# Holding the weight loads of an attention + MLP kernel behind the third pair's k, with a re-measured schedule model

## The chip, the cores and the metric

The kernel runs on one core of a Trainium2 chip. The metric is device time in microseconds (us) of that core; lower is better. "Span" is the length of the one execution that was profiled; a run's time is about 1.7 us longer than its span. A run is called slow when it is more than 1.5% above the fastest run of the same kernel, otherwise fast.

In the profile lines PE is TensorE's matmuls, PEld its weight loads, DVE VectorE, ACT ScalarE, POOL GpSimd and SP the Sync engine. PEclk is the granted clock: the share of TensorE's full clock that the records show. The DMA share is the mean busy share of the core's 16 DMA engines as the profile counts it; it passes 1 here (1.24 from 11 to 12 us of the kernel before).

## The reference

Block-sparse attention (4 batches, 8 heads, 768 tokens, head size 64) is followed by a two-layer MLP with a gated activation. Inputs and outputs are fp32.

```python
def _attn_ref(q, k, v, sampled_blocks):        # q, k, v: (4, 8, 768, 64)
    scores = scale * np.matmul(q, k.transpose(0, 1, 3, 2))
    mask = ...                                  # neighbours, first and last blocks, 3 sampled blocks of 32
    scores = np.where(mask, scores, -1e9)
    ...                                         # softmax over keys
    return np.matmul(attn, v)

def _moe_ref(x, w_in, w_out, beta):             # x: (3072, 512), w_in: (512, 2048), w_out: (2048, 512)
    h = x @ w_in
    g = h * (1.0 / (1.0 + np.exp(-beta * h)))
    return g @ w_out
```

## The kernel before

The kernel works on pairs of heads. There are 16 pairs: four per batch. Per pair, k, q and v are loaded as fp32 by the Sync engine's hardware DMA queue, cast to fp16 by VectorE or GpSimd, and k and q are transposed ("turned"): for pairs 0 to 3 on TensorE, later by DMA. TensorE makes scores, ScalarE takes exponentials, VectorE applies the mask, TensorE multiplies by v. When a stretch of tokens is complete for all four pairs, the MLP follows: `w_in` matmuls (up-projection), tanh, product, `w_out` matmuls (down-projection).

The weights are 8.4 MB of fp32. GpSimd issues four loads of 2.1 MB each that also cast to fp16 (4.2 MB written). They go through the software DMA queue.

The emitted order is not written by hand. A list scheduler in Python (`order_of`) simulates engines, buffers and two DMA "wires" with constants of its own, and emits each engine's instructions in the order in which its model starts them. A constant of the model has an effect only by moving instructions.

```python
BIAS = {"mask": -29, ..., "load": 168, "cast": 123, "dma": -234, ...}   # (cut) priority offsets, ns
RATE = {"SP": 356.0, "POOL": 410.0}              # bytes per ns of the two wires
DMA_FIRST = {"SP": 1260.0, "POOL": 2000.0}       # ns from issue to first byte
SHARED = 60.0                                    # what SP gets while both run

    def add_weights(after):                      # after: a load of the second pair
        for i in range(2):
            def wi(i=i):
                nc.gpsimd.dma_start(out=w_in_sb[:, :, i * 1024:(i + 1) * 1024],
                                    in_=w_in_r[:, :, i * 1024:(i + 1) * 1024])
            w_in_of[i] = add("weights", "POOL", 1000, 0, wi,
                            deps=[after, (mask_of[1], -1e9)], moved=2097152, port=True)
        ...                                      # two more for w_out
    # later loads: k of pair 4 waits for w_out's first half, its q and v for the second half
    for x in range(NPAIR, len(pairs)):
        add_prep(x, (0, 1, 1) if x == NPAIR else (None, None, None))
```

The `after` dependency exists only in the model. Nothing in the emitted program makes GpSimd wait for that load, so the weight loads go out as soon as GpSimd gets to them: from 8.36 us in the trace before, right behind its three mask copies (7.01 to 8.42 us). Pairs 0 to 3 load k, the first 256 columns of q, then v; the rest of q for these four pairs is loaded after all of that.

The softmax here doesn't subtract the row's maximum and nothing guards it: scores larger than these inputs give would overflow.

Of the kernel before, what the change touches and what calls it, by code (L numbers as in the profile page):

```python
# [23 lines left out]
class Node:  # L24


    def __init__(self, kind, eng, dur, lat, emit, deps=(), take=(), use=(), moved=0,
# [10 lines left out]
        self.start = self.done = self.on = None  # L38


BIAS = {"mask": -29, "spread": 107, "beta": 401, "weights": 209, "load": 168, "cast": 123,
        "dma": -234, "turn": 72, "turn cp": 164, "sc": -30, "next sc": -209, "lone sc": 110,
        "ex": 138, "mk": 62, "av": 35, "norm": 5, "x turn": 26, "x cp": 78, "hp": 33, "op": 68,
        "op on": 83, "th": 123, "gm": -192, "osb": 149}

HOP = 60.0
SWITCH = 100.0
RATE = {"SP": 356.0, "POOL": 410.0}
DMA_FIRST = {"SP": 1260.0, "POOL": 2000.0}
DMA_LAST = 900.0  # L50
SHARED = 60.0

# [1 line left out]
def order_of(nodes, free, slots):  # L54

    free = dict(free)
    give = {p: [(0.0, s) for s in range(n)] for p, n in slots.items()}
    rows = 128
    wire = {"SP": 0.0, "POOL": 0.0}
    port = {"DVE": 0.0, "POOL": 0.0}  # L60
    left, after, at_dep = {}, {}, {}
    todo = []
    for n in nodes:
        left[n] = len(n.deps)
        at_dep[n] = n.at
        for d, x in n.deps:
            after.setdefault(d, []).append((n, x))
        if not n.deps:
            todo.append(n)
    out = []  # L70
    while todo:
        best = None
        for n in todo:
            ready = at_dep[n]
            want = {}
            for b in n.take:
                want[b.pool] = want.get(b.pool, 0) + 1
            ok = True
            for p, c in want.items():
                if len(give[p]) < c:  # L80
                    ok = False
                    break
                ready = max(ready, sorted(give[p])[c - 1][0])
            if not ok:
                continue
            for e in n.eng:
                n_start = max(ready, free[e])
                if n.port and e in port:
                    n_start = max(n_start, port["POOL" if e == "DVE" else "DVE"])
                bias = BIAS[n.kind]  # L90
                if n.rows == 64:
                    if rows == 64:
                        bias += BIAS["next sc"]
                    elif sum(t <= n_start for t, _ in give["sc"]) < 2:
                        bias += BIAS["lone sc"]
                key = (n_start + n.dur[e] - min(n.dur.values()) + bias, n.place)
                if best is None or key < best[0]:
                    best = (key, n, e, n_start)
        if best is None:
            raise RuntimeError("no node can start")  # L100
        _, n, e, start = best
        if e == "PE" and n.rows != rows:
            start, rows = start + SWITCH, n.rows
        n.on, n.start = e, start
        free[e] = start + n.dur[e]
        if n.port and e in port:
            port[e] = free[e]
        if n.moved:
            other = "POOL" if e == "SP" else "SP"
            t, rest, rate = max(wire[e], start + DMA_FIRST[e]), n.moved, RATE[e]  # L110
            if wire[other] > t:
                if e == "POOL":
                    t = wire[other]
                else:
                    both = min(rest, (wire[other] - t) * SHARED)
                    wire[other] += both / RATE[other]
                    t, rest = t + both / SHARED, rest - both
            wire[e] = t + rest / rate
            n.done = wire[e] + DMA_LAST
        else:  # L120
            n.done = free[e] + n.tail
        for b in n.take:
            t, b.slot = min(give[b.pool])
            give[b.pool].remove((t, b.slot))
        for b in n.use:
            b.users -= 1
            b.end = max(b.end, n.done)
            if b.users == 0:
                give[b.pool].append((b.end + HOP, b.slot))
        todo.remove(n)  # L130
        out.append(n)
        for m, x in after.get(n, ()):
            at_dep[m] = max(at_dep[m], n.done + HOP + x)
            left[m] -= 1
            if left[m] == 0:
                todo.append(m)
    if len(out) < len(nodes):
        raise RuntimeError("some nodes never become ready")
    return out
# [3 lines left out]
def kernel(  # L143
# [192 lines left out]
    N_PE_TURN = 4  # L336
    prep = {}

    w_in_of, w_out_of = {}, {}
    last_load = []  # L340

    def add_weights(after):
        for i in range(2):
            def wi(i=i):
                nc.gpsimd.dma_start(out=w_in_sb[:, :, i * 1024:(i + 1) * 1024],
                                    in_=w_in_r[:, :, i * 1024:(i + 1) * 1024])
            w_in_of[i] = add("weights", "POOL", 1000, 0, wi,
                            deps=[after, (mask_of[1], -1e9)], moved=2097152, port=True)
        for i in range(2):
            def wo(i=i):  # L350
                nc.gpsimd.dma_start(out=w_out_sb[:, i * 8:(i + 1) * 8, :],
                                    in_=w_out_r[:, i * 8:(i + 1) * 8, :])
            w_out_of[i] = add("weights", "POOL", 1200, 0, wo, deps=[(w_in_of[1], -1e9)],
                              moved=2097152, port=True)
# [4 lines left out]
    def add_load(nm, x, st, lo, hi, gate):  # L359
        b, j = pairs[x]  # L360
        src = {"k": k, "q": q, "v": v}[nm]

        def load():
            hg = src[b, 2 * j:2 * j + 2].rearrange("h (g p c) d -> p (h g) (c d)", g=NG, p=P)
            o = at(st).rearrange("p h (g c) -> p (h g) c", g=NG)
            if hi - lo == NC:
                nc.sync.dma_start(out=o, in_=hg)  # L367
            else:
                for g in range(lo // CG, hi // CG):
                    nc.sync.dma_start(out=o[:, g::NG], in_=hg[:, g::NG])  # L370
        deps = [(last_load[0], -1e9)] if last_load else []
        kw = {"take": [st]}
        if gate is not None:
            def shut():
                nc.gpsimd.tensor_copy(out=at(st)[0:1, 0, lo * D:lo * D + 1],
                                      in_=w_out_sb[0:1, gate * 8, 0:1])
            deps.append(add("weights", "POOL", 150, 50, shut, deps=[w_out_of[gate]], take=[st]))
            kw = {"use": [st]}
        last_load[:] = [add("load", "SP", 500 if hi - lo in (NC, CG) else 1000, 0, load, deps=deps,
                             moved=65536 * (hi - lo) + (500000 if x == 0 and nm == "v" else 0),  # L380
                             **kw)]
        return last_load[0]

    def add_cast(x, nm, st, dst, lo, hi, load):
        w = (hi - lo) * P

        def cast(eng):
            e = nc.vector.tensor_copy if eng == "DVE" else nc.gpsimd.tensor_copy
            src = at(st)[:, :, lo * D:hi * D].rearrange("p h (c d) -> p h c d", d=D)
            e(out=at(dst)[:, :, :, 0:D] if nm == "v" else by_chunk(dst, lo, hi),  # L390
              in_=src)
        return add("cast", ("DVE", "POOL"), {"DVE": 60 + 0.53 * w, "POOL": 50 + 0.94 * w}, 90, cast,
                   deps=[load], take=[dst], use=[st], port=True)

    def add_half(x, nm, kq, lo, hi, first, gate):

# [1 line left out]
        w = (hi - lo) * P  # L398
        st, s16 = Buf(f"st_{nm}"), Buf(f"s16_{nm}")
        load = add_load(nm, x, st, lo, hi, gate)  # L400
        c = add_cast(x, nm, st, s16, lo, hi, load)
        if x >= N_PE_TURN:
            def turn():
# [19 lines left out]
    def add_prep(x, gates=(None, None, None)):  # L423
        kq, va, st = Buf("set"), Buf("va"), Buf("st_v")
        hi = Q1 // P if x < NPAIR else NC
        tk = add_half(x, "k", kq, 0, NC, None, gates[0])
        tq = add_half(x, "q", kq, 0, hi, tk, gates[1])
        lv = add_load("v", x, st, 0, NC, gates[2])
        cv = add_cast(x, "v", st, va, 0, NC, lv)
        prep[x] = {"kq": kq, "va": va, "k": tk, "q": tq, "q on": tq, "v": cv}  # L430
        return lv

    def add_rest(x):
        r = prep[x]
# [41 lines left out]
    def add_step(step):  # L476
        x, q0, sc, et, mm, ex, mk, masks = step
        r = prep[x]
        g = add("sc", "PE", 218, 180, mm, deps=[r["k"], r["q"] if q0 == 0 else r["q on"]],
                take=[sc], use=[r["kq"]], rows=64)  # L480
        e = add("ex", "ACT", 927, 100, ex, deps=[g], take=[et], use=[sc])
        return add("mk", "DVE", 612, 80, mk, deps=[e] + masks, use=[et], port=True)
# [118 lines left out]

    n_bh = add_mask()

    at_load = [add_prep(x) for x in range(NPAIR)]
    add_weights(at_load[1])
    for x in range(NPAIR):
        add_rest(x)
    for x in range(NPAIR, len(pairs)):
# [63 lines left out]
```

## Time and profile before

| | before |
|---|---|
| time, median of the runs first given | 307.5 us (305.45 to 307.69) |
| span of the profiled run | 303.9 us |
| TensorE busy | 269.2 us, so 34.7 us idle |
| TensorE busy in the first 40 us | 15.5 us |
| first `w_in` matmul | 51.5 us |

First the page of the kernel before: its span, the busy times, and two rows in 40 slices of 7.6 us (TensorE's busy tenths; the DMA share in tenths).

```profile
span 303.9 us, 6163 instructions
...
PE 269.2 (89%) x2455; PEld 140.8 (46%) x2455; DVE 211.2 (69%) x427; ACT 212.4 (70%) x276; POOL 31.8 (10%) x48
...
PE   5714079999987999998999999999999999999995
...
DMA  7999958519999996677212620112101111002002
...
```

TensorE is at 7 to 9 from the sixth slice on, and at 9 almost everywhere after the thirteenth. The holes are in slices 1 to 5, and there the DMA row is at 7 to 9. So the start waits for DMA and the rest is bound by TensorE.

The waits before 60 us (engine and its line, what released it, total us, times, longest):

```profile
...
engine line waited for: us in total, times, longest us
POOL s_q L390 <- DMA st_q<-in_q_dram: 28.4, 1, 28.4
ACT et L461 <- PE sc L453: 16.4, 5, 13.6
...
PE mm L412 <- DVE s_q L390: 11.9, 3, 8.2
...
```

Stretches of the kernel before: start and end in us, length, busy us of each engine with its number of instructions, granted clock, DMA share, GB/s.

```profile
...
core 0: us, PE busy (x) PEld busy (x) DVE busy (x) ACT busy (x) POOL busy (x), PEclk, DMA share, GB/s
10.00:11.00 1.00, 0.31 (x4) 0.21 (x3) 1.00 (x3) 0.36 (x1) 1.00 (x2) 1.00 1.22 291
11.00:12.00 1.00, 0.77 (x16) 0.71 (x14) 1.00 (x3) 0.00 (x0) 1.00 (x2) 1.00 1.24 266
12.00:13.00 1.00, 1.00 (x17) 1.00 (x15) 1.00 (x3) 0.00 (x0) 0.18 (x1) 1.00 1.12 218
...
30.00:35.00 5.00, 0.00 (x0) 0.00 (x0) 0.56 (x1) 0.00 (x0) 0.00 (x0) 1.00 1.20 215
0.00:40.00 40.00, 15.49 (x133) 9.52 (x135) 15.86 (x46) 12.13 (x15) 8.88 (x22) 1.00 1.08 223
...
```

The DMA moves about 290 GB/s until 11 us and 215 to 218 GB/s after 12 us. The change of level marks the moment at which weight traffic joins (these GB/s count written bytes; the page's software queue has 4.19 MB for the 8.4 MB of fp32 weights). Between 30 and 35 us TensorE does nothing.

Next, one v load, pair 3's (the tile view, limited to what is issued from 10.3 to 11.2 us), and the weights (the tile view of `w_in_sb` up to 75 us; each line gives count, durations, first and last start):

```profile
...
L367 SPq DMA_DIRECT2D st_v<-in_v_dram x1: 415/415/415, 10.8 to 10.8; - x1
...
DMA to landing us min/median/max: 20.4/20.4/20.4
```

```profile
...
L554 PE MATMUL mm<-xT_sb,w_in_sb x64: 269/273/283, 51.5 to 60.9; 128*128 128x256 f16 x64
L345 POOL DMA_DIRECT2D w_in_sb<-in_moe_w_in_dram x2: 748/833/918, 8.4 to 9.3; - x2
...
DMA to landing us min/median/max: 10.3/12.9/15.4
```

Pair 3's v needed 20.4 us from issue at 10.8 us to landing at 31.2 us, because it shares the DMA with the weights, which were issued from 8.4 us on. The `w_in` halves landed at 18.7 and 24.7 us, but the first `w_in` matmul comes at 51.5 us. The weights came early, and the data that the attention needs first came late.

### The profile page before, as it was taken

To read this page: it belongs to the slowest core of one execution; us is meant where nothing else is said; L and a number is where in the kernel's file an instruction comes from. 1 tells how busy PE (TensorE), PEld (TensorE's weight loads), DVE (VectorE), ACT (ScalarE), POOL (GpSimd) and SP (SyncE) were. 2 spreads that over 40 slices of the span, in tenths; PEclk is the share of its full clock that TensorE was granted. 3 is DMA by queue.
4 is the path that set the end of the run, shared out by engine and by line. 5 is a ranking of instruction groups with operands and counts; after the bars stand their busy time and mean duration, and the time that the engine had idled before them with its cause. 6 is when DMAs were issued, how large, how long until landed. Compare 5 with 4: busy or idle time off the path is not lost.

```text
span 303.9 us, 6163 instructions
## 1 busy us (share of the span) xinstructions
PE 269.2 (89%) x2455; PEld 140.8 (46%) x2455; DVE 211.2 (69%) x427; ACT 212.4 (70%) x276; POOL 31.8 (10%) x48
## 2 busy tenths in 40 slices
PE   5714079999987999998999999999999999999995
PEld 2503035665532536543645446455336364465742
DVE  5812169889985958897967778678887588762510
ACT  2533058999886668699788877787997689734621
POOL 5600032101133110123300001000000000000000
PEclk9999999999999999999999999999999999999999
DMA  7999958519999996677212620112101111002002
GB/s 211 256 216 215 217 167 214 125 35 279 242 273 257 250 266 112 144 159 175 71 28 73 112 42 19 52 54 85 22 0 38 35 69 38 8 11 78 37 36 105
DMA packets 72850, 36.66 MB, mean 121 GB/s; under 512 B 29796, under 2 KB 68724, under 8 KB 72820
## 3 DMA queue, kind: packets, MB, share of 16 engines
q1 hardware_dynamic: 69568, 32.06, 44.7%
q0 software_dynamic: 3136, 4.19, 7.7%
q8 instruction: 19, 0.31, 0.4%
q14 instruction: 11, 0.09, 0.1%
q10 hardware_dynamic: 116, 0.01, 0.0%
HBM read 27.27 MB, written 6.29 MB: 110 GB/s over the span
## 4 chain that ended last, share of the span: by engine, by line
PE 68%; DMA 11%; DVE 9%; SPq 5%; ACT 5%; issue 1%; DVEq 0%; ACTq 0%
PE mm L578 26%; PE mm L554 21%; PE mm L504 11%; PE sc L453 10%; DMA st_q<-in_q_dram 5%; DMA qX<-s_q 5%; SPq L370 4%; DVE et L470 4%; ACT et L461 4%; DVE g L563 2%; DMA sb_i<-in_sampled_blocks_dram 1%; DVE s_q L390 1%; ACT t_sb L559 1%; SPq L404 1%; SPq L367 1%
## 5 line engine op out<-in xcount | busy, mean ns | idle before, releaser
L461 ACT ACTIVATE et<-sc 128x1024 f16<-128x1024 f32 x144 | 141.3, 1029 | 39.2 <-PE sc L453 37.9
L470 DVE TENSOR_TENSOR et<-et,mask 128x1024 f16<-128x1024 f16 x144 | 100.6, 705 | 24.7 <-ACT et L461 24.4
L554 PE MATMUL mm<-xT_sb,w_in_sb 128*128 128x512 f16 (+1 forms) x448 | 90.8, 349 | 4.1 <-DVE g L563 3.7
L578 PE MATMUL mm<-w_out_sb,g 128*128 128x512 f16 x384 | 93.3, 380 | 0.0
L559 ACT ACTIVATE t_sb<-mm,beta_h_sb 128x512 f16<-128x512 f32 (+1 forms) x112 | 68.0, 645 | 19.4 <-PE mm L554 18.6
L563 DVE SCALAR_TENSOR_TENSOR g<-t_sb,mm 128x512 f16<-128x512 f16 (+1 forms) x112 | 65.4, 607 | 19.2 <-ACT t_sb L559 18.8
L554 PEld LDWEIGHTS <-w_in_sb 128*128 128x128 f16 x448 | 42.0, 98 | 48.8 <-issue 12.6
L578 PEld LDWEIGHTS <-g 128*128 128x128 f16 x384 | 33.8, 98 | 43.9 <-issue 11.6
L453 PE MATMUL sc<-qX,kX 64*128 64x256 f16 (+1 forms) x384 | 49.3, 350 | 3.9 <-ACT et L461 2.6
L504 PEld LDWEIGHTS <-et 128*128 128x128 f16 x1152 | 42.7, 100 | 10.1 <-issue 2.9
L504 PE MATMUL mm<-va,et 128*128 128x65 f16 x1152 | 44.8, 197 | 1.7 <-DVE va L390 1.5
L453 PEld LDWEIGHTS <-kX 64*128 64x128 f16 x384 | 15.9, 97 | 27.4 <-issue 23.5
L514 DVE TENSOR_TENSOR xst<-mm,recip 128x256 f16<-128x256 f32 x48 | 19.8, 418 | 0.5
L588 ACT ACTIVATE osb<-mm 128x512 f32<-128x512 f32 x11 | 6.6, 599 | 15.4 <-PE mm L578 15.2
L390 DVE CAST s_q<-st_q 128x768 f16<-128x768 f32 (+2 forms) x12 | 5.8, 487 | 14.0 <-DMA st_q<-in_q_dram 8.0
L412 PE MATMUL mm<-identity,s_q 128*128 128x128 f16 x24 | 4.0, 306 | 11.9 <-DVE s_q L390 11.9
L390 POOL CAST s_q<-st_q 128x768 f16<-128x768 f32 (+2 forms) x8 | 6.4, 804 | 65.7 <-DMA st_q<-in_q_dram 42.8
L390 POOL CAST va<-st_v 128x768 f16<-128x768 f32 x8 | 7.5, 959 | 52.7 <-PE mm L504 41.8
L390 POOL CAST s_k<-st_k 128x768 f16<-128x768 f32 x9 | 8.9, 991 | 34.9 <-DMA kX<-s_k 31.5
L511 DVE RECIPROCAL recip<-mm 128x4 f32<-128x4 f32 x48 | 8.3, 176 | 5.0 <-PE mm L504 4.6
L412 PE MATMUL mm<-identity,s_k 128*128 128x128 f16 x24 | 3.3, 310 | 8.2 <-DVE s_k L390 6.3
L417 ACT COPY kX<-mm 128x768 f16<-128x768 f16 x3 | 2.4, 798 | 10.9 <-PE mm L412 10.9
(52 smaller groups left out, 54.6 us busy)
## 6 DMA issues: line engine op xcount, KB each, us to landing
st_k<-in_k_dram SPq DMA_DIRECT2D x16, 384.0 KB, 5.1
st_v<-in_v_dram SPq DMA_DIRECT2D x16, 384.0 KB, 6.0
out_dram<-osb SPq DMA_DIRECT2D x24, 256.0 KB, 2.0
st_q<-in_q_dram SPq DMA_DIRECT2D x12, 384.0 KB, 5.1
w_in_sb<-in_moe_w_in_dram POOLq DMA_DIRECT2D x2, 1024.0 KB, 12.9
w_out_sb<-in_moe_w_out_dram POOLq DMA_DIRECT2D x2, 1024.0 KB, 25.7
st_q<-in_q_dram SPq DMA_DIRECT2D x12, 128.0 KB, 14.6
xT_sb<-xst SPq DMA_TRANSPOSE x22, 2.4
```

The source lines that it names most:

```text
L370: nc.sync.dma_start(out=o[:, g::NG], in_=hg[:, g::NG])
L390: e(out=at(dst)[:, :, :, 0:D] if nm == "v" else by_chunk(dst, lo, hi), in_=src)
L453: nc.tensor.matmul(at(sc)[:, hh, i * n:(i + 1) * n], lhsT=kX[hh * D:(hh + 1) * D, (kc0 + i) * P:(kc0 + i + 1) * P], rhs=qX[hh * D:(hh + 1) ...
L461: nc.scalar.activation(out=at(et).rearrange("p h q -> p (h q)"), in_=at(sc).rearrange("p h q -> p (h q)"), func=AF.Exp, bias=0.0, scale=SCALE)
L470: nc.vector.tensor_tensor(out=e, in0=e, in1=m, op=ALU.mult)
L504: nc.tensor.matmul(a[:, i, hh, :], lhsT=at(ets[kc // kn])[:, hh, at0:at0 + P], rhs=at(va)[:, hh, kc, 0:D + 1], start=(kc == 0), stop=(kc = ...
L511: nc.vector.reciprocal(out=at(rb), in_=av_ap()[:, :, :, D:D + 1])
L514: nc.vector.tensor_tensor(out=at(xs)[:, half * 2:half * 2 + 2], in0=av_ap()[:, :, :, 0:D], in1=at(rb).to_broadcast([P, 2, 2, D]), op=ALU.mult)
L554: nc.tensor.matmul(at(hb)[:, 0:n], lhsT=w_in_sb[:, c, f * P:(f + 1) * P], rhs=xT_sb[:, c, t0:t0 + n], start=(c == 0), stop=(c == NPAIR - 1))
L559: nc.scalar.activation(out=at(tb)[:, 0:n], in_=at(hb)[:, 0:n], func=AF.Tanh, bias=0.0, scale=beta_h_sb[:, f:f + 1])
L563: nc.vector.scalar_tensor_tensor(out=at(gb)[:, f, 0:n], in0=at(tb)[:, 0:n], scalar=1.0, in1=at(hb)[:, 0:n], op0=ALU.add, op1=ALU.mult)
L578: nc.tensor.matmul(at(ob), lhsT=at(gb)[:, f, ts * P:(ts + 1) * P], rhs=w_out_sb[:, f, :], start=(f == 0), stop=(f == N_FFC - 1))
```

## The change

The intent is to hold the weight loads until the third pair's k (pair 2) has landed. GpSimd first copies one element of that pair's staged k into `w_in_sb`; in the trace after, the copy waits 2.09 us for the load, and the weight DMA waits 0.31 us for the copy. The schedule model gets new constants (software-queue delay 2.0 to 4.2 us; sync rate 356 to 305), gets a slack (spare time) of 1.5 us on steps that DMA feeds, and its biases are re-tuned. It also charges the small copies that gate later loads with 600 ns instead of 150.

```diff
-BIAS = {"mask": -29, "spread": 107, ... }
+BIAS = {"mask": -288, "spread": 115, ... }                 (all values re-tuned, cut)
+W_GATE = (2, "k")
+SLACK = 1500.0
-RATE = {"SP": 356.0, "POOL": 410.0}
-DMA_FIRST = {"SP": 1260.0, "POOL": 2000.0}
+RATE = {"SP": 305.0, "POOL": 410.0}
+DMA_FIRST = {"SP": 1260.0, "POOL": 4200.0}
 ...
-    def add_weights(after):
+    def add_weights(gate):
+        st, load = gate
+        def shut():
+            nc.gpsimd.tensor_copy(out=w_in_sb[0:1, 0, 0:1], in_=at(st)[0:1, 0, 0:1])
+        gate = add("weights", "POOL", 600, 50, shut, deps=[load], use=[st])
 ...
-                            deps=[after, (mask_of[1], -1e9)], moved=2097152, port=True)
+                            deps=[gate if i == 0 else (w_in_of[0], -1e9)], moved=2097152, port=True)
 ...                                                         (casts of pairs 4.. and scores of
                                                              pairs with DMA transposes:)
-                   deps=[load], ...
+                   deps=[(load, SLACK if x >= NPAIR else 0)], ...
```

The model also no longer delays weight traffic behind sync traffic that was issued before it (one branch removed).

More of the change, by code (lines that the diff above doesn't have):

```diff
@@ L38, in __init__ @@
         self.start = self.done = self.on = None
-BIAS = {"mask": -29, "spread": 107, "beta": 401, "weights": 209, "load": 168, "cast": 123,
-        "dma": -234, "turn": 72, "turn cp": 164, "sc": -30, "next sc": -209, "lone sc": 110,
-        "ex": 138, "mk": 62, "av": 35, "norm": 5, "x turn": 26, "x cp": 78, "hp": 33, "op": 68,
-        "op on": 83, "th": 123, "gm": -192, "osb": 149}
+BIAS = {"mask": -288, "spread": 115, "beta": 289, "weights": 285, "load": 963, "cast": 110,
+        "dma": -659, "turn": 69, "turn cp": 125, "sc": -30, "next sc": -293, "lone sc": 106,
+        "ex": 240, "mk": 63, "av": 40, "norm": 9, "x turn": 37, "x cp": -282, "hp": 31, "op": 57,
+        "op on": 82, "th": 187, "gm": -28, "osb": 157}
+W_GATE = (2, "k")
+SLACK = 1500.0
 HOP = 60.0
 SWITCH = 100.0
-RATE = {"SP": 356.0, "POOL": 410.0}
-DMA_FIRST = {"SP": 1260.0, "POOL": 2000.0}
+RATE = {"SP": 305.0, "POOL": 410.0}
+DMA_FIRST = {"SP": 1260.0, "POOL": 4200.0}
 DMA_LAST = 900.0
@@ L110, in order_of @@
             t, rest, rate = max(wire[e], start + DMA_FIRST[e]), n.moved, RATE[e]
-            if wire[other] > t:
-                if e == "POOL":
-                    t = wire[other]
-                else:
-                    both = min(rest, (wire[other] - t) * SHARED)
-                    wire[other] += both / RATE[other]
-                    t, rest = t + both / SHARED, rest - both
+            if e == "SP" and wire[other] > t:
+                both = min(rest, (wire[other] - t) * SHARED)
+                wire[other] += both / RATE[other]
+                t, rest = t + both / SHARED, rest - both
             wire[e] = t + rest / rate
@@ L337 @@
     prep = {}
-    w_in_of, w_out_of = {}, {}
+    w_in_of, w_out_of, loads = {}, {}, {}
     last_load = []
-    def add_weights(after):
+    def add_weights(gate):
[3 more added lines that the diff above has]
+        gate = add("weights", "POOL", 600, 50, shut, deps=[load], use=[st])
         for i in range(2):
@@ L376, in shut @@
                                       in_=w_out_sb[0:1, gate * 8, 0:1])
-            deps.append(add("weights", "POOL", 150, 50, shut, deps=[w_out_of[gate]], take=[st]))
+            deps.append(add("weights", "POOL", 600, 50, shut, deps=[w_out_of[gate]], take=[st]))
             kw = {"use": [st]}
@@ L392, in add_cast @@
         return add("cast", ("DVE", "POOL"), {"DVE": 60 + 0.53 * w, "POOL": 50 + 0.94 * w}, 90, cast,
-                   deps=[load], take=[dst], use=[st], port=True)
+                   deps=[(load, SLACK if x >= NPAIR else 0)], take=[dst], use=[st], port=True)
     def add_half(x, nm, kq, lo, hi, first, gate):
@@ L400, in add_half @@
         load = add_load(nm, x, st, lo, hi, gate)
+        if x < NPAIR and lo == 0:
+            loads[x, nm] = st, load
         c = add_cast(x, nm, st, s16, lo, hi, load)
@@ L430, in add_prep @@
         prep[x] = {"kq": kq, "va": va, "k": tk, "q": tq, "q on": tq, "v": cv}
-        return lv
+        if x < NPAIR:
+            loads[x, "v"] = st, lv
     def add_rest(x):
@@ L478, in add_step @@
         r = prep[x]
-        g = add("sc", "PE", 218, 180, mm, deps=[r["k"], r["q"] if q0 == 0 else r["q on"]],
+        g = add("sc", "PE", 218, 180, mm, deps=[(r["k"], SLACK if x >= N_PE_TURN else 0),
+                      (r["q"] if q0 == 0 else r["q on"], SLACK if x >= N_PE_TURN else 0)],
                 take=[sc], use=[r["kq"]], rows=64)
@@ L602 @@
     n_bh = add_mask()
-    at_load = [add_prep(x) for x in range(NPAIR)]
-    add_weights(at_load[1])
+    for x in range(NPAIR):
+        add_prep(x)
+    add_weights(loads[W_GATE])
     for x in range(NPAIR):
```

## The prediction

> **What bounds the kernel now.** Span 303.9 us (median time 307.5). By stretches, TensorE is busy 98.8 of 100 us after 100 us and 100.3 of the last 104, at granted clock 1.00: that part is TensorE-bound. Its 35 us of idle (303.9 - 269.2) lie mostly at the start: busy 15.5 of the first 40 us, 0 from 30 to 35. There the DMA is full (share above 1 from 5 to 40 us). Waits before 60 us: ScalarE 13.6 us for scores, GpSimd 28.4 for a q load, TensorE 8.2 for a q cast.
>
> Why: the weight loads are issued at 8.4 to 12.2 us. Sync-queue loads land at about 290 GB/s until pair 2's v (13.0 us), then crawl: pair 3's k took 9.6 us more (393 KB, 41 GB/s) to 22.6, its q 25.0, its v 31.2; the rests of q (262 KB each) 35.0, 38.8, 40.5, 41.2. So weight traffic begins about 12.5 us, 4.2 us after its first issue. [...]
>
> **What the change does.** Same bytes, same matmuls. A 1x1 GpSimd copy (0.2 to 0.65 us by its siblings) reads pair 2's staged k (landing 9.9 to 11.7), so first weight issue 8.4 -> about 12 us, flow 12.5 -> 16. Meanwhile the sync queue moves about 1 MB: pair 3's k, q, v (917 KB) land by about 16.5 us. The q rests follow at about 65 GB/s: 20.5, 24.5, 29, 33. Weights: w_in 18.7/24.7 -> 22/28; w_out 32.6/39.9 -> 36/41. The DMA front still ends near 41 us; only the order changes. In the emitted order TensorE no longer puts pair 3's k transpose ahead of pair 2's scores, and the first w_in matmuls come after 17 exps instead of 19. Slack should remove some later waits for transposed q (about 5 us of chain at 80, 92 and 136 us, though TensorE idles only 4 us in 60 to 100).
>
> **How much is critical.** Twelve first-tile exps (0.95 us each) from 7.5 us end by about 21; five more wait for q rests until about 29; first w_in matmul about 31 us instead of 51.5. That is 20 us earlier with two exps (2 us) less done: 18 gained. w_out (41 us) comes before its need (63.5 - 18 = 45). Batch 1's loads stay gated by w_out (about 42 us; 41.8 before) while its first exp is wanted at about 58 instead of 76.7: I charge 3 us for new waits, and credit 2 for slack.
>
> Gain about 17 us: span about 287, time 290 us, range 284 to 298. Faster by over 2%: 0.94; within 2%: 0.05; slower: 0.01.
>
> **What would show it.** Right: w_in issue at 11 to 13 us; pair 3's v landed by 18; no empty TensorE slice at 30 to 38 us; first w_in matmul before 35; TensorE busy near 269, idle near 18. Wrong: pair 3's loads landing past 22 us; w_out after 45 with down-projection waiting; new TensorE or ScalarE waits on transposed q/k between 45 and 90 us.
>
> **What would make it wrong.** TensorE stalls behind a q-rest transpose (pair 2's is ahead of the first w_in matmul); batch 1's loads cannot follow a pipeline 18 us ahead; re-tuned order worse later.

The forecast's sum: 20 us earlier, less 2 for exponentials left to do, less 3 for new waits, plus 2 for slack, is a gain of 17 us.

## The result, and the profile after

Ratios in this document are the mean time of one kernel's fast runs over that of the other's fast runs of the same rounds, so they are not quite the ratio of the medians quoted.

The changed kernel took 290.14 us (288.8 to 291.47, 4 runs); the kernel before took 306.96 us in the same comparison. The ratio is 0.9458, 95% interval 0.9394 to 0.9522. The span in the profiled run was 287.6 us.

The page after, the same lines (slices of 7.2 us):

```profile
span 287.6 us, 6162 instructions
...
PE 265.2 (92%) x2455; PEld 138.1 (48%) x2455; DVE 209.4 (73%) x429; ACT 212.9 (74%) x277; POOL 27.6 (10%) x46
...
PE   4767899979895999899999999999999999999994
...
DMA  7999987999999997771227201021002111011112
...
```

The holes of slices 3 to 5 (1, 4 and 0 tenths) are at 6 to 8 now. The DMA row is as full at the start as it was. Waits before 60 us:

```profile
...
POOL s_q L394 <- PE mm L562: 16.5, 1, 16.5
...
ACT et L468 <- PE sc L460: 8.6, 8, 4.4
...
DVE s_q L394 <- DMA st_q<-in_q_dram: 1.4, 1, 1.4
...
```

ScalarE's wait for scores fell from 16.4 to 8.6 us. GpSimd's longest wait is now for TensorE, at no cost that these lines show. Stretches:

```profile
...
14.00:15.00 1.00, 1.00 (x12) 0.74 (x9) 0.04 (x1) 1.00 (x2) 0.04 (x1) 1.00 1.23 289
15.00:16.00 1.00, 1.00 (x9) 0.37 (x7) 0.39 (x2) 0.88 (x1) 0.94 (x2) 1.00 1.28 277
16.00:17.00 1.00, 0.42 (x6) 0.21 (x5) 1.00 (x3) 0.91 (x1) 1.00 (x2) 1.00 1.11 214
...
30.00:35.00 5.00, 4.55 (x40) 3.12 (x40) 4.85 (x12) 4.50 (x10) 0.61 (x1) 1.00 1.23 213
0.00:40.00 40.00, 29.55 (x287) 18.47 (x288) 30.70 (x85) 28.79 (x42) 10.48 (x25) 0.96 1.10 231
...
```

The drop of the throughput now comes just before 16 us instead of between 11 and 12 us. TensorE is busy 29.55 us in the first 40 instead of 15.49, a gain of 14.1 us. The gate itself in GpSimd's timeline (start, duration), then pair 3's v and the weights:

```profile
...
11.31 0.75 POOL L345 CAST w_in_sb<-st_k 1x1 f16<-1x1 f32 x1 [2.09 <-DMA st_k<-in_k_dram]
12.38 0.92 POOL L349 DMA_DIRECT2D w_in_sb<-in_moe_w_in_dram  x1 [0.31 <-POOL w_in_sb L345]
```

```profile
...
L371 SPq DMA_DIRECT2D st_v<-in_v_dram x1: 415/415/415, 10.8 to 10.8; - x1
...
DMA to landing us min/median/max: 5.4/5.4/5.4
```

```profile
...
L562 PE MATMUL mm<-xT_sb,w_in_sb x103: 269/273/390, 30.7 to 74.9; 128*128 128x256 f16 x64, 128*128 128x512 f16 x39
L349 POOL DMA_DIRECT2D w_in_sb<-in_moe_w_in_dram x2: 746/832/918, 12.4 to 13.3; - x2
...
DMA to landing us min/median/max: 10.8/13.2/15.7
```

Pair 3's v lands 5.4 us after issue, at 16.2 us. The first `w_in` matmul runs at 30.7 us, 20.8 us earlier, although `w_in` now lands at 23.2 and 29.0 us, that is, 4.3 to 4.5 us later than before. The later part is not wholly free. TensorE is busy 34.0 us between 60 and 100 us, against 35.95 us in the kernel before, and one new wait stands out in the timeline:

```profile
...
88.72 0.56 DVE L394 CAST va<-st_v 128x768 f16<-128x768 f32 x1 [4.72 <-DMA st_v<-in_v_dram]
...
89.20 0.42 DVE L522 TENSOR_TENSOR xst<-mm,recip 128x256 f16<-128x256 f32 x1
...
89.67 0.38 PE L586 MATMUL mm<-w_out_sb,g 128*128 128x512 f16 x1 [3.27 <-DVE xst L522]
...
```

VectorE had a v cast next in its order and waited 4.72 us for that v load. The normalisation step behind it on the same engine was ready to go (TensorE, which makes its input, had last run at 86.4 us), and TensorE waited 3.27 us for that step.

### The profile page after: what moved, and what is told of

The parts are those of the page before. It is cut to its first block, busy times and chain, and to the rows that moved or that the text cites. A ratio compares the mean times of both kernels' runs of the same rounds, so it can differ in the third digit from the quotient of the medians.

```text
span 287.6 us, 6162 instructions
## 1 busy us (share of the span) xinstructions
PE 265.2 (92%) x2455; PEld 138.1 (48%) x2455; DVE 209.4 (73%) x429; ACT 212.9 (74%) x277; POOL 27.6 (10%) x46
## 4 chain that ended last, share of the span: by engine, by line
PE 71%; DMA 13%; DVE 7%; SPq 3%; ACT 2%; issue 1%; POOL 0%; DVEq 0%; POOLq 0%; ACTq 0%
PE mm L586 27%; PE mm L562 24%; PE mm L512 10%; PE sc L460 10%; DMA st_q<-in_q_dram 9%; DVE et L477 3%; ACT et L468 2%; DMA kX<-s_k 2%; SPq L410 1%; DMA sb_i<-in_sampled_blocks_dram 1%; DMA st_k<-in_k_dram 1%; SPq L374 1%; DVE g L571 1%; DVE s_k L394 1%; SPq L371 1%
## 5 line engine op out<-in xcount | busy, mean ns | idle before, releaser
L562 PE MATMUL mm<-xT_sb,w_in_sb 128*128 128x512 f16 (+1 forms) x448 | 90.7, 349 | 2.8 <-DVE g L571 2.3
L567 ACT ACTIVATE t_sb<-mm,beta_h_sb 128x512 f16<-128x512 f32 (+1 forms) x112 | 67.4, 635 | 15.7 <-PE mm L562 15.2
L571 DVE SCALAR_TENSOR_TENSOR g<-t_sb,mm 128x512 f16<-128x512 f16 (+1 forms) x112 | 65.2, 606 | 18.1 <-ACT t_sb L567 17.6
L562 PEld LDWEIGHTS <-w_in_sb 128*128 128x128 f16 x448 | 42.2, 98 | 47.6 <-issue 11.2
L460 PE MATMUL sc<-qX,kX 64*128 64x256 f16 (+1 forms) x384 | 47.3, 338 | 5.0 <-ACT et L468 3.0
L512 PEld LDWEIGHTS <-et 128*128 128x128 f16 x1152 | 41.1, 99 | 8.4 <-issue 1.2
L512 PE MATMUL mm<-va,et 128*128 128x65 f16 x1152 | 43.3, 195 | 1.0 <-DVE osb L598 0.7
L460 PEld LDWEIGHTS <-kX 64*128 64x128 f16 x384 | 15.2, 95 | 28.8 <-issue 23.1
L596 ACT ACTIVATE osb<-mm 128x512 f32<-128x512 f32 x14 | 8.4, 599 | 16.5 <-PE mm L586 16.3
L394 POOL CAST s_q<-st_q 128x768 f16<-128x768 f32 (+2 forms) x9 | 7.5, 835 | 38.5 <-PE mm L562 16.5
L394 POOL CAST s_k<-st_k 128x768 f16<-128x768 f32 x7 | 5.8, 830 | 45.3 <-DMA st_k<-in_k_dram 26.3
L394 DVE CAST va<-st_v 128x768 f16<-128x768 f32 x10 | 5.8, 576 | 5.8 <-DMA st_v<-in_v_dram 5.8
L394 POOL CAST va<-st_v 128x768 f16<-128x768 f32 x6 | 5.5, 920 | 30.7 <-PE mm L512 23.1
L598 DVE TENSOR_SCALAR osb<-mm 128x512 f32<-128x512 f32 x10 | 6.8, 685 | 0.0
L540 DVE COPY xT_sb<-mm 128x256 f16<-128x256 f16 (+1 forms) x10 | 3.6, 357 | 4.3 <-PE mm L535 4.3
## 6 DMA issues: line engine op xcount, KB each, us to landing
w_out_sb<-in_moe_w_out_dram POOLq DMA_DIRECT2D x2, 1024.0 KB, 22.2
```

Source lines behind the costliest of these rows:

```text
L394: e(out=at(dst)[:, :, :, 0:D] if nm == "v" else by_chunk(dst, lo, hi), in_=src)
L460: nc.tensor.matmul(at(sc)[:, hh, i * n:(i + 1) * n], lhsT=kX[hh * D:(hh + 1) * D, (kc0 + i) * P:(kc0 + i + 1) * P], rhs=qX[hh * D:(hh + 1) ...
L512: nc.tensor.matmul(a[:, i, hh, :], lhsT=at(ets[kc // kn])[:, hh, at0:at0 + P], rhs=at(va)[:, hh, kc, 0:D + 1], start=(kc == 0), stop=(kc = ...
L562: nc.tensor.matmul(at(hb)[:, 0:n], lhsT=w_in_sb[:, c, f * P:(f + 1) * P], rhs=xT_sb[:, c, t0:t0 + n], start=(c == 0), stop=(c == NPAIR - 1))
L567: nc.scalar.activation(out=at(tb)[:, 0:n], in_=at(hb)[:, 0:n], func=AF.Tanh, bias=0.0, scale=beta_h_sb[:, f:f + 1])
L571: nc.vector.scalar_tensor_tensor(out=at(gb)[:, f, 0:n], in0=at(tb)[:, 0:n], scalar=1.0, in1=at(hb)[:, 0:n], op0=ALU.add, op1=ALU.mult)
```

## The experiments

Two theories were to be told apart. Theory A: the gain comes from holding back the weight traffic. Theory B: it comes from the new instruction order, and the gate does little. After these, the questions were how long to hold, what the model's constants are worth, and what the new waits after 45 us cost. All results were correct. For om, p3v and n6 there are two traces: figures are from the first (spans 292.2, 296.0 and 341.3 us) unless the second is named (295.8, 293.1 and 284.4 us).

| label | what it is | median us of all runs (range) | ratio to before, fast runs |
|---|---|---|---|
| (the change) | gate on pair 2's k, new order | 290.14 (288.8 to 291.47) | 0.9458 |
| a1 | the change again | 291.02 (290.51 to 292.18) | 0.9513 |
| g0 | new order, gate does not wait | 297.96 (295.75 to 300.13) | 0.9777 |
| m1 | no gate, planned anew | 304.17 (299.53 to 305.26) | none given |
| g1 | old order, gate added | 294.77 (294.1 to 295.17) | 0.967 |
| om | gate in the model, old constants | 294.94 (293.86 to 296.62) | 0.9675 |
| s0 | slack 0, planned anew | 291.37 (289.78 to 293.94) | 0.9569 |
| gv3 | new order, gate on pair 3's v | 287.9 (287.13 to 290.72) | 0.9414 |
| p3v | planned anew for pair 3's v | 296.12 (295.05 to 297.72) | 0.9701 |
| c2v | v casts on GpSimd only | 291.28 (289.73 to 293.27) | 0.9516 |
| c1 | pair 4's q, v loads earlier | 290.94 (289.21 to 292.44) | 0.9493 |
| n6k | TensorE turns pairs 4 and 5 too | 289.37 (287.29 to 290.61) | 0.9423 |
| n6 | p3v and those turns | 285.48 (283.35 to 343.07) | 0.9338 |

g0, m1, g1 and s0 shared their runs of the kernel before (305.49 us); so did a1, gv3, c2v and c1 (306.04 us), and om, p3v and n6 (305.69 us). n6k ran against 306.75 us.

### The new order without the wait (g0_no_wait_new_order)

Every engine's order is that of the change. Only what the copy waits for is taken away.

```diff
-nc.gpsimd.tensor_copy(out=w_in_sb[0:1, 0, 0:1], in_=at(st)[0:1, 0, 0:1])
+nc.gpsimd.tensor_copy(out=w_in_sb[0:1, 0, 0:1], in_=identity[0:1, 0:1])
```

> The changed kernel in its own emitted order, but the gating copy reads the identity tile, so it waits for nothing that is late. Theory A (holding back the weight traffic is what gains): w_in is issued at about 9.4 us instead of 12.4, traffic begins about 13.5, pair 3's v lands at 25 us or later, pair 2's second part of q near 37 us, the first w_in matmul near 38 us instead of 30.7; about 297 us, ratio to before about 0.968. Theory B (the new order gains, the gate does little): about 290 us, ratio about 0.946, first w_in matmul still near 31 us.

Measured: 297.96 us, ratio 0.9777 (0.9674 to 0.988). In the tile view the first `w_in` matmul moved to 40.6 us, and pair 3's v landed at 28.2 us. The stretches from 25 to 35 us show TensorE idle again:

```profile
...
L371 SPq DMA_DIRECT2D st_v<-in_v_dram x1: 415/415/415, 11.1 to 11.1; - x1
...
DMA to landing us min/median/max: 17.1/17.1/17.1
...
L562 PE MATMUL mm<-xT_sb,w_in_sb x68: 269/272/389, 40.6 to 74.9; 128*128 128x256 f16 x64, 128*128 128x512 f16 x4
...
```

```profile
...
25.00:30.00 5.00, 0.00 (x0) 0.00 (x0) 0.56 (x1) 0.00 (x0) 0.00 (x0) 0.54 1.19 214
30.00:35.00 5.00, 2.19 (x14) 1.06 (x15) 2.15 (x6) 1.73 (x3) 0.00 (x0) 0.50 1.20 215
...
```

The granted clock reads 0.54 and 0.50 in these two lines; in the kernel before it reads 1.00 through the 5 us from 30 us without a matmul. The mean clock alone does not give the time: in the rounds of g0 the kernel before took 301.68 and 305.48 us at 1.000, and 305.66 us at 0.943.

A moved the way it said, by a little more than forecast. About half of the change's gain is lost by taking away one wait of GpSimd, with nothing else touched. B in its strong form falls. But 297.96 is still 7.5 us below the 305.49 us of the kernel before (the interval lies below 1, though not clear of the 2% line). The order by itself is not quite isolated here: in g0 the weights go out at 10.0 us, 1.6 us later than in the kernel before, so part of the 7.5 us may be a short hold again.

### No gate anywhere (m1_replanned_no_gate)

```diff
-        gate = add("weights", "POOL", 600, 50, shut, deps=[load], use=[st])
+        gate = load
-                            deps=[gate if i == 0 else (w_in_of[0], -1e9)], ...
+                            deps=[(mask_of[1], -1e9) if i == 0 else (w_in_of[0], -1e9)], ...
```

> No gate in the kernel nor in the schedule model; everything else of the change kept and the order planned anew for it. Theory A: as the run above, ratio 0.96 to 0.98. Theory B: 0.946 to 0.955.

Measured: 304.17, 305.26, 304.18 and 299.53 us. By the rule above the first three count as slow beside the fourth, so no ratio was given; their granted clocks (0.954 to 0.966) do not set them apart. Even the fastest is 9 us above the change. The first `w_in` matmul came at 44.9 us. This one plan of the new model, made for a world without the gate, gained little or nothing.

### The old order with the gate (g1_gate_old_order)

```diff
             def wi(i=i):
+                if i == 0:
+                    nc.gpsimd.tensor_copy(out=w_in_sb[0:1, 0, 0:1],
+                                          in_=T["st_k"][2][0:1, 0, 0:1])
                 nc.gpsimd.dma_start(...)
```

> The kernel before, in its own emitted order, with only the gating copy added ahead of the first w_in load. Theory A: w_in issue about 12 us, pair 3's v landed by 17 us, first w_in matmul about 33 us instead of 51.5, about 292 us, ratio about 0.952. Theory B: the old order keeps its stalls, ratio 0.99 to 1.00.

Measured: 294.77 us, ratio 0.967 (0.9603 to 0.9738). One copy of one element, added to the kernel before and nothing else, gains 10.7 us. The issue came at 12.2 us and pair 3's v landed at 16.3 us, as A said, but the first `w_in` matmul came at 37.8 us and not at 33:

```profile
...
L557 PE MATMUL mm<-xT_sb,w_in_sb x82: 269/273/390, 37.8 to 74.9; 128*128 128x256 f16 x64, 128*128 128x512 f16 x18
...
```

The reason is in VectorE's timeline:

```profile
...
25.13 0.43 DVE L393 CAST s_q<-st_q 128x512 f16<-128x512 f32 x1 [5.67 <-DMA st_q<-in_q_dram]
25.48 0.68 DVE L473 TENSOR_TENSOR et<-et,mask 128x1024 f16<-128x1024 f16 x1
```

VectorE, in the old order, has the cast of a second part of q placed ahead of a mask multiply. It waited 5.67 us for that load, and the multiply, whose exponentials had ended at 20.8 us, stood behind it until 25.5 us; ScalarE waited 5.7 us for scores and TensorE 4.6 us for the cast. The new order has these casts nearer to where the data arrives: its longest such wait before 60 us is 1.4 us. That is the part of the order's contribution that the traces show; no run moved this one cast alone.

### Slack zero (s0_slack_zero)

```diff
-SLACK = 1500.0
+SLACK = 0.0
```

> The changed kernel with the slack on DMA-fed steps set to 0 and the order planned anew. My forecast credited slack with 2 us: about 292 us, ratio about 0.952, with more waits on transposed q or k between 45 and 140 us. If slack does nothing: 0.946. If it is a main part of the gain: 0.97 or more.

Measured: 291.37 us, ratio 0.9569 (0.948 to 0.9658). The change itself took 290.14 and, later, 291.02 us. A difference of at most about 1 us, in other rounds, is not resolved. My credit of 2 us for slack is not confirmed, and nothing here supports slack as a main part of the gain. Both rest on one new plan (see p3v below).

### The yardstick again (a1_change_again)

No edit.

> The changed kernel again, as the yardstick of these rounds: 290 us, ratio about 0.95 to the kernel before, first w_in matmul at 30.7 us.

Measured: 291.02 us, ratio 0.9513 (0.9483 to 0.9543), first `w_in` matmul at 32.0 us.

### Holding longer in the same order (gv3_hold_longer)

```diff
-... in_=at(st)[0:1, 0, 0:1])
+... in_=T["st_v"][0][0:1, 0, 0:1])      # at this point: pair 3's v
```

> The changed kernel in its own order, the gating copy reading pair 3's v (landing 16.2 us) instead of pair 2's k. Holding-back theory: w_in issue about 17.5 us, traffic from about 21.5, all of q landed by about 21 us, w_in landed about 28 and 34 us, first w_in matmul 28 to 29 us; but the DMA idles about 1 us near 21 us and w_out and all later loads come 1 to 2 us later, so the gain has saturated: 288 to 292 us, within 1% of the change. If more holding were still better in proportion (13 us for the first 3 us of hold): under 285 us. If weights are what matters early: over 295 us.

Measured: 287.9 us, ratio 0.9414 (0.9375 to 0.9453), against 0.9513 for the change in the same rounds: 3 us faster, with intervals that do not overlap. The median lies just below the range of 288 to 292 us that I gave.

```profile
...
L562 PE MATMUL mm<-xT_sb,w_in_sb x111: 270/273/390, 28.9 to 75.0; 128*128 128x256 f16 x64, 128*128 128x512 f16 x47
L349 POOL DMA_DIRECT2D w_in_sb<-in_moe_w_in_dram x2: 748/884/1020, 17.6 to 18.6; - x2
...
```

```profile
...
19.00:20.00 1.00, 0.33 (x9) 0.20 (x6) 0.97 (x4) 0.68 (x1) 1.00 (x3) 1.00 0.85 58
20.00:21.00 1.00, 0.67 (x10) 0.40 (x8) 0.62 (x3) 0.61 (x1) 1.00 (x3) 1.00 0.66 100
100.00:140.00 40.00, 38.38 (x406) 20.56 (x403) 32.86 (x63) 32.30 (x42) 4.87 (x6) 1.00 0.73 143
...
```

The issue moved to 17.6 us and the first `w_in` matmul to 28.9 us. In issue times, the step from g0 (10.0 us) to a1 (12.0 us) gained 7 us, and the next 5.6 us of hold gained 3 us: it saturates. From 19 to 21 us the DMA moves only 58 and 100 GB/s (share 0.85 and 0.66), which is the price of the hold.

Whether the change stopped too early is less sure than the intervals suggest. TensorE's idle time is no shorter in gv3's trace (22.2 us) than in those of the change (22.4) and of a1 (21.0). What is shorter is its busy time for the same 2455 matmuls: 263.2 against 265.2 and 269.5 us, at mean granted clocks of 1.000, 0.994 and 0.971. The change's own four runs took 288.8 and 289.3 us at 0.993 and 0.994, and 291.0 and 291.5 us at 0.975. So part of the 3 us may be the clock. Near 0.98 the two overlap less clearly: gv3 took 287.8 and 290.7 us, a1 290.9 and 291.1 us. Whether the longer hold keeps the clock up, or this is chance, was not tested.

### Planned for the longer hold (p3v_planned_for_v3)

```diff
-W_GATE = (2, "k")
+W_GATE = (3, "v")
```

> The changed kernel with the gate moved from pair 2's k to pair 3's v in the kernel and in the model, the order planned anew. The same gate without new planning took 287.9 us (ratio 0.941). If planning for the gate adds what it seemed to add before: 285 us, 0.933. If the order is only noise of a per cent: 287 to 290 us, and the longer hold is confirmed by a second order.

Measured: 296.12 us, ratio 0.9701 (0.965 to 0.9753). Both forecasts missed it. The hold worked as in gv3 (issue 17.2 us, first `w_in` matmul 31.4 us, TensorE busy 29.3 us in the first 40). In this trace TensorE's largest shortfall is later, where the gate has long been passed:

```profile
...
100.00:140.00 40.00, 33.41 (x315) 16.81 (x316) 31.83 (x61) 28.65 (x37) 3.66 (x4) 0.96 0.84 187
...
```

TensorE is busy 33.4 of these 40 us, and 38.4 in gv3 (last line of its fence above). The second trace of p3v has 36.4 us there, so this stage differs between runs. Over that whole trace TensorE idles 24.0 us against 22.2 in gv3, but it is busy 269.1 against 263.2 us for the same matmuls, at a mean clock of 0.982 against 1.000. Most of the difference is thus not idle time; what lengthens the busy time, the lower clock or less overlap between matmuls, is not shown. The same gate in two orders differs by 8 us. So the planner, given a slightly different problem, can be 8 us better or worse by its order alone, and a difference of less than that between two kernels that were each planned anew does not show what their edit does. This limits m1, s0, om, c1, c2v, n6 and n6k.

### The gate with the old constants (om_old_model_with_gate)

The change with the old biases, `RATE`, `DMA_FIRST`, the old branch for shared wires, and `SLACK = 0`; the gate stays in model and kernel.

```diff
-RATE = {"SP": 305.0, ...};  DMA_FIRST = {..., "POOL": 4200.0};  SLACK = 1500.0
+RATE = {"SP": 356.0, ...};  DMA_FIRST = {..., "POOL": 2000.0};  SLACK = 0.0   (and the old BIAS)
```

> The gate both in the kernel and in the schedule model, but the model with its old constants (software-queue delay 2.0 us, sync rate 356, old biases, no slack) and the order planned anew. If the measured delay and the new constants are what make the new order good: near the old order with the gate, about 295 us, ratio 0.965. If planning with the gate in the model is enough: near the change, 291 us, 0.951.

Measured: 294.94 us, ratio 0.9675, which is g1's 294.77 us. It also has g1's 5.7 us wait of VectorE for a q load, and the first `w_in` matmul at 37.8 us (second trace: longest wait 6.8 us, first matmul at 40.5 us). Telling the old model of the gate brought nothing in this plan, and the new constants together came out about 4 us better. That is less than the 8 us between two plans (p3v), so it is not shown that the constants do it, nor which of them.

### The v casts on GpSimd (c2v_v_casts_on_gpsimd)

```diff
-        return add("cast", ("DVE", "POOL"), ...
+        return add("cast", ("POOL",) if x >= NPAIR and nm == "v" else ("DVE", "POOL"), ...
```

> The changed kernel, planned anew with the v casts of pairs 4 to 15 on GpSimd only. The changed kernel lost 3.3 us of TensorE at 86 to 90 us behind a VectorE cast that waited 4.7 us for a v load. If such head-of-line waits on VectorE are the new waits that I charged with 3 us: that wait goes and the time falls by 2 to 3 us, to about 287.5 us (ratio to the change 0.99). If DMA throughput between 55 and 100 us sets the pace, the wait only moves: 290 us.

Measured: 291.28 us, ratio 0.9516, the same as the change (0.9513). The 3.3 us wait is gone, but the stretches from 60 to 140 us, first of the change and then of this kernel, show what happened:

```profile
...
60.00:100.00 40.00, 34.04 (x305) 15.72 (x303) 30.34 (x59) 29.73 (x37) 9.14 (x10) 1.00 1.21 243
100.00:140.00 40.00, 38.82 (x433) 21.27 (x430) 34.08 (x67) 32.39 (x41) 4.85 (x6) 1.00 0.72 157
...
```

```profile
...
60.00:100.00 40.00, 37.97 (x354) 18.40 (x351) 33.66 (x65) 33.86 (x42) 8.48 (x8) 1.00 1.16 243
100.00:140.00 40.00, 36.08 (x372) 19.18 (x372) 30.72 (x60) 29.11 (x37) 6.74 (x7) 0.96 0.71 151
...
```

From 60 to 100 us TensorE gained 3.9 us of busy time, and from 100 to 140 us it lost 2.7. As the second theory had it, the wait moved. Whether DMA supply or this order moved it, the run does not tell.

### Pair 4's q and v earlier (c1_batch1_loads_earlier)

```diff
-        add_prep(x, (0, 1, 1) if x == NPAIR else (None, None, None))
+        add_prep(x, (0, 0, 0) if x == NPAIR else (None, None, None))
```

> The changed kernel, planned anew with pair 4's q and v gated by the first half of w_out (landing 35.3 us) as its k is, instead of the second half (40.8 us). If the DMA-bound stretch from 50 to 100 us costs the new waits: loads start 5 us earlier, about 1.5 us faster than the change (0.995), w_out's second half about 3 us later without a wait. If w_out's second half is needed at once: slower by 1 to 3 us.

Measured: 290.94 us, ratio 0.9493 (0.9456 to 0.9531). This is not told apart from the change. Inconclusive.

### Two more pairs turned on TensorE (n6_two_more_pe_turns, n6k_turns_with_2k_gate)

```diff
-    N_PE_TURN = 4
+    N_PE_TURN = 6          # n6: with W_GATE = (3, "v");  n6k: with W_GATE = (2, "k") as in the change
```

> As the run above, and the k and q of pairs 4 and 5 turned on TensorE instead of by DMA, to take DMA work out of the DMA-bound stretch from 50 to 100 us. If DMA throughput there sets the pace of what is left: 2 to 3 us faster than the run above. If TensorE and its copies pay it back[...]: the same or 1 to 2 us slower.

> The change itself (gate on pair 2's k) with only the k and q of pairs 4 and 5 turned on TensorE instead of by DMA, planned anew. The kernel with the later gate and the same turns took about 284.7 us in its fast runs. If the turns on TensorE are what gained there (less DMA work and fewer landings to wait for between 45 and 140 us): 285 to 287 us here too, ratio about 0.935 to 0.94, TensorE waits in 50 to 140 us down. If it was the later gate, or that one plan: 290 to 292 us, 0.95. A run in a state of low granted clock over the whole execution (one of six there) may come again.

n6 measured 284.66, 286.31, 284.59 and 283.35 us in its fast runs, ratio 0.9338 (0.9276 to 0.9401), the best of all. Two of its six runs were slow: 287.67 us, and one of 343.07 us at a mean granted clock of 0.757. That last one was profiled first (it shows 0.75 in every stretch from 40 us to the end, and no run here explains it); the second trace (span 284.4 us, clock 0.998) is of a fast execution. Its fast runs (median 284.6 us) gain about 11 us over p3v, not the 2 to 3 us forecast. In the second traces of both, TensorE idles 17.4 us instead of 24.0, and all of that difference lies between 40 and 140 us (busy 97.4 against 90.7 us). Gone are p3v's waits after 40 us for ScalarE (3.9 us) and for one VectorE copy (3.0 us). That is about where the edit aimed, but the order was planned anew as well, and which of the two did it is not shown. n6k measured 289.37 us, ratio 0.9423 (0.9384 to 0.9462), between the two forecasts: the turns alone gave at most 1% over the change, and the low clock did not come again in its six runs (0.980 to 0.993). n6 beats both kernels in its fast runs; before one used it, one would have to know how often it falls to that clock.

## Why the prediction was right

The time was forecast at 290 us and measured at 290.14; the span at 287 and measured at 287.6. Point by point:

| step | forecast | measured |
|---|---|---|
| first weight issue | 12 us | 12.38 us |
| pair 3's k, q, v all landed | 16.5 us | 16.2 us |
| `w_in` landed | 22, 28 us | 23.2, 29.0 us |
| `w_out` landed | 36, 41 us | 35.3, 40.8 us |
| first `w_in` matmul | 31 us | 30.7 us |
| from there to the end of the span | 3 us longer (2 for exponentials left to do, 3 charged for waits, 2 credited to slack) | 4.5 us longer (252.4 to 256.9) |
| TensorE busy, idle | 269, 18 us | 265.2, 22.4 us |

The mechanism and the early steps were right. That the total came within 1 us is partly luck. Idle time was forecast 4.4 us too low and busy time 3.8 us too high, and the two errors cancel; a1, the same kernel, had 269.5 us busy and 21.0 idle, and took 291.02 us.

**Conservation of DMA bytes was the right tool.** The DMA was full before and stayed full up to 41 us (mean share 1.05 and 1.08 of that stretch). The change could only exchange what comes first, and the landing times of the table follow from two rates that the trace before shows: 290 GB/s alone, about 65 GB/s for the sync queue beside the weights. The DMA view of that trace, cut to a window, shows how the second rate arises, which I had overlooked. The two queues moved equal numbers of packets: from 15 to 20 us 436 of the sync queue (0.22 MB) and 435 of the weights (0.86 MB written), from 30 to 35 us 724 and 724 (0.35 and 0.73 MB). The sync queue's packets were the smaller ones (about 0.5 KB, against 2.0 and 1.0 KB), so it got the smaller share, 44 and 70 GB/s. g0 and g1 show the cause. In g0, with only the wait taken away, in the same order, pair 3's v lands at 28.2 instead of 16.2 us, the first `w_in` matmul comes 9.9 us later in the traces, and the time rises by 7 to 8 us. In g1 the copy alone, in the old order, gains 10.7 us.

**The rival was partly right, and my prediction gave it too little.** I argued nearly the whole 18 us from landing times. In the runs the gate gives 10.7 us in the old order (305.49 to 294.77). The rest, about 4 us, needs the new order (g1's 294.77 against 290.14 and 291.02, from other rounds). The two effects are not simply additive: g0, the new order without the wait, gains 7.5 us, with its weights issued 1.6 us later than before.

**I named the wrong instruction for the order's part.** I wrote that TensorE "no longer puts pair 3's k transpose ahead of pair 2's scores". g1 keeps that placing, and with the gate it costs nearly nothing, because pair 3's k is there at 14.4 us. What cost 5.7 us in g1 was a q cast at the head of VectorE's queue. My forecast for g1, 292 us, missed by about that effect.

**The late terms were about right in sum and wrong in kind.** I charged 3 us for new waits on transposed q or k, and credited 2 us to slack. The new wait of 3.3 us was for a v load, behind a VectorE cast. The credit for slack was not confirmed (s0). That removing this wait gains nothing in time (c2v, planned anew) the forecast had not foreseen.

**The software-queue delay was over-read.** I put the start of weight traffic at 12.5 us, 4.2 us after issue. In stretches of 1 us, the one in which the throughput falls has 266 GB/s in the kernel before (11 to 12 us, between levels of 291 and 218) and 277 in the changed one (15 to 16 us, between 289 and 214). Taken as a mix of the two levels, the fall comes at about 11.7 and 15.8 us, so 3.3 us after the issue at 8.36 us and 3.5 us after 12.38 us. In the DMA view the first packets of the software queue lie at 11.1 to 11.2 and at 15.2 to 15.3 us, 2.7 to 2.9 us after the issue. The shift between the kernels, which is what my sum used, was right all the same.

## What to carry to other kernels

When a stretch is bound by DMA bytes, ask which bytes are needed first, and make the program hold the others back: here a dependency that existed only in the schedule model held nothing (first weight issue at 8.4 us), while a one-element copy that reads the awaited tile and writes into the destination did (12.2 us in g1, 12.4 us in the change). Then look at the order within each engine: on VectorE, a cast that waited for a load (5.7 us in g1, 4.7 us in the change) held up work behind it whose data was ready. Test such a part with the instruction order fixed; two automatically planned orders of nearly the same problem differed by 8 us here, more than most of the edits did.
